# Moving the 64-row matmuls of a fused RWKV-7 and feed-forward kernel next to other 64-row work

## The chip, the cores and the metric

The kernel runs on one core of a Trainium2 chip. The metric is the device time of one execution in microseconds; for the kernel before, three runs gave 839.8, 840.27 and 841.61 us, and the median, 840.27 us, is the time before. All times of single instructions come from one profiled execution of 840.4 us.

A core has five engines with a queue each: TensorE (PE; its weight loads are listed apart as PEld), VectorE (DVE), ScalarE (ACT), GpSimd (POOL) and SyncE (SP), which here issues the DMA transfers. They meet at semaphores. Products of TensorE land in PSUM[...].

## The reference

```python
for t in range(S):                      # S = 768 steps; state is B, H, D, D = 4, 8, 40, 40
    y[:, :, t] = einsum('bhd,bhde->bhe', rt, state)
    Sa = einsum('bhde,bhe->bhd', state, at)
    state = state * wt[:, :, None, :] - einsum('bhd,bhe->bhde', Sa, bt)
    state = state + einsum('bhd,bhe->bhde', vt, kt)
x = y.transpose(0, 2, 1, 3).reshape(3072, 320)
h = x @ w_in                            # 320 x 2048
g = h * clip(h + 3, 0, 6) / 6
out = g @ w_out                         # 2048 x 320
```

The inputs r, k, v, w, a, b are fp32; the two weight matrices come in as 64-bit floats and the kernel makes fp32 of them itself.

## The kernel before, in words

**Units and groups.** The recurrence is computed in blocks of 64 steps. A *unit* is one block of one pair of batch elements, all 8 heads: 128 tokens, with the 64 steps of one batch element in partitions 0 to 63 and those of the other in 64 to 127. There are 24 units (`NK`), and four of them (`NU`: two blocks of two pairs) are a *group*. Within a block the recurrence is turned into products of small matrices: a triangular matrix of every head is inverted once per group (VectorE, lines 660 and 666, in steps that `aside` deals out), and the state of 40 x 40 per head goes from block to block. Its sums with the products of a block are the stage `sn` (matmuls in line 864, addition on VectorE in line 873).

**Stages.** `prepare` and `step` give each unit's work as stages, such as `W`, `A`, `B`, `K` (transposes), `E` and `EV` of the preparation, and `RT`, `VT`, `R`, `C`, `U`, `UT`, `rS`, `sn`, `H`, `y` of the step. A stage issues its matmuls, yields, and then issues what ScalarE, VectorE and GpSimd make of the products. From the third group on, and in the step from the second, transposes are done as *half turns*: 64 rows at a time (`turn_halves`, line 430; line 570 for the factors). Most other products of the stages use 64 rows and 64 columns of the array, or 40 rows of one such part; those of the inversion use 32 x 32 (lines 696 and 719).

**The feed-forward.** The outputs of a unit are moved by DMA into a tile `xt` of 320 features by 128 tokens, cut as 128 + 128 + 64 features. The generator `feed_forward` runs through 48 *jobs*, two for each unit, with 1024 hidden features each. A job has two parts. `expand` fills two PSUM banks `h` (c = 0 and 1, four chunks of 128 hidden features each) with 16 matmuls of 128 rows (line 968) in four pieces, and then with 8 *short* matmuls of 64 rows for the last 64 features (line 973, alternately in the upper and the lower half of the array); then ScalarE makes relu(h + 3) of each bank (line 978), and VectorE makes min of it and 6 times h (line 979, tile `gt`), which frees the bank. `contract` multiplies the result by the second weight matrix: 8 matmuls with 320 columns of output (line 992), in four pieces of two. The order is expand of one job, contract of the job before, expand of the next. There are two banks `h`, both held by one job, one bank `o` for the output and five banks `any` for the stages.

**Who sets the order.** The kernel writes its order out by hand; each engine's queue runs in it. The last loop (from the fourth unit on) goes through four rounds of stages per unit. In each, `a_block` collects the stages that are due, in two parts, and `together` issues all their matmuls in the order of the list `PRODUCTS`, then all their results in the order of `RESULTS`. The first three entries of `PRODUCTS`, `W`, `S` and `K` (the list `TURNS`), are transposes with all 128 rows; the fourth, `RT`, is a half turn. Between the parts `feed` calls `pieces(n)`, which adds up fractions and takes a whole piece from `feed_forward` whenever one is owed; a job is nine pieces, five of `expand` and four of `contract`. What is left after the last stage is taken piece by piece.

**The first group** is done differently, by `by_twos` and then by a plan written out line by line. At the same time the weights are converted in 20 pieces on VectorE and ScalarE (lines 299 to 328), and the state of the four units is summed there for the first time.

Of the kernel before, what the change touches and what calls it, by code (L numbers as in the profile page):

```python
# [16 lines left out]
P = 128  # L17
# [3 lines left out]
SLOT = 64  # L21
# [8 lines left out]
def kernel(  # L30
# [42 lines left out]
    nc = tc.nc  # L73
    B, H, T, D = r.shape
# [3 lines left out]
    NU = 2 * NP  # L78
# [12 lines left out]
    ffn = ctx.enter_context(tc.tile_pool(name="ffn", bufs=1))  # L91
# [3 lines left out]
    def bank(tag, shape, bufs):  # L95
        return ps.tile(shape, F32, name=tag, tag=tag, bufs=bufs)
# [11 lines left out]
    def ps_pair(*dims):  # L108

        n = 1  # L110
        for d in dims:
            n *= d
        if shared[0] is None or shared[1] + n > 512:
            shared[:] = [ps_any([P, 512]) for _ in range(2)], 0
        at = shared[1]
        shared[1] += n
        views, step = [], n
        for d in dims:
            step //= d
            views.append([step, d])  # L120
        return [_ap(t[:], at, views) for t in shared[0]]
# [6 lines left out]
        out=ident[:], in_=ones, pattern=[[1, P]],  # L128
# [4 lines left out]
        out=ones[:, 0:BL], in_=ones[:, 0:BL], pattern=[[1, BL]],  # L133
# [314 lines left out]
    def half(i, n=SLOT):  # L448
        return slice(SLOT * i, SLOT * i + n)
# [285 lines left out]
    def step(i):  # L735
# [117 lines left out]
                nc.scalar.activation(out=ys[:, rs::2], in_=ysp[rs], func=AF.Copy)  # L853

        def s_sn():
            sn = ps_pair(NPR, D)
            for name in "KB":
                for pr in range(NPR):
                    for s in range(2):
                        for q in range(2):  # L860
                            h = 2 * pr + s
                            by = VN[half(q), 4 * s + pr, 0:D] if name == "K" else \
                                m["U"][half(q), 4 * (s ^ q) + pr, 0:D]
                            nc.tensor.matmul(  # L864
                                out=sn[q][half(s, D), pr, :],
                                lhsT=o[name][half(q), h * D:(h + 1) * D], rhs=by,
                                start=(name == "K" and pr == 0), stop=(name == "B" and pr == NPR - 1),
                            )
            yield PE
            for q in range(2):  # L870
                for s in range(2):
                    x = st[half(s, D), q, :, 0:D]
                    nc.vector.tensor_tensor(out=x, in0=sn[q][half(s, D)], in1=x, op=ALU.add)  # L873

        def s_H():
            x = scores(m["UT"], m["RT"], swap=True)
# [58 lines left out]
    jobs = deque([(i, r) for r in range(2) for i in range(SPLIT)])  # L935
    jobs.extend((i, r) for i in range(SPLIT, NK) for r in range(2))
    sums = {}

    def available():
        if not jobs:  # L940
# [4 lines left out]
    def feed_forward():  # L945

        last = None
        while True:
            while not available():
                if last:  # L950
                    yield from contract(*last)
                    last = None
                yield None
            i, r = jobs.popleft()
            gts = []
            yield from expand(ready[i], r * NQ, gts)
            if last:
                yield from contract(*last)
            last = (i, r, gts)

    def expand(xt, j0, gts):

        hp = [bank("h", [P, NQ, P], 2) for _ in range(2)]
        for c in range(2):
            for t in range(2):
                for i in range(NQ):
                    j = c * HJ + j0 + i
                    nc.tensor.matmul(out=hp[c][:, i, :], lhsT=win[:, t, j * P:(j + 1) * P],  # L968
                                     rhs=xt[:, t, :], start=(t == 0 and i == 0), stop=False)
                yield True  # L970
        for i in range(NQ):
            for c in range(2):
                nc.tensor.matmul(out=hp[c][:, i, :],  # L973
                                 lhsT=win2[half(c), (j0 + i) * P:(j0 + i + 1) * P],
                                 rhs=xt[half(c), 2, :], start=False, stop=(i == NQ - 1))
        for c in range(2):
            gt = ffn.tile([P, NQ, P], F32, name="gt", bufs=5)
            nc.scalar.activation(out=gt[:], in_=hp[c][:], func=AF.Relu, bias=three[:], scale=1.0)  # L978
            nc.vector.scalar_tensor_tensor(out=gt[:], in0=gt[:], scalar=6.0, in1=hp[c][:],  # L979
                                           op0=ALU.min, op1=ALU.mult)  # L980
            gts.append(gt)
        yield True

    def contract(i, r, gts):
        split = i < SPLIT
        if r == 0 or split:
            op = bank("o", [P, DM], 1)
        else:
            op = sums.pop(i)
        for c in range(2):  # L990
            for n in range(NQ):
                nc.tensor.matmul(out=op[:], lhsT=gts[c][:, n, :],  # L992
                                 rhs=wout[:, c * HJ + r * NQ + n, :],
                                 start=((split or r == 0) and c == 0 and n == 0),
                                 stop=((split or r == 1) and c == 1 and n == NQ - 1))
                if n % 2 and (c == 0 or n < NQ - 1):
                    yield True
        if r == 0:
            sums[i] = op
            if split:  # L1000
                part = ffn.tile([P, 3 * P], F32, name="part", tag="xt", bufs=6)[:, 0:DM]
                nc.scalar.activation(out=part, in_=op[:], func=AF.Copy, scale=1.0 / 6.0)
                sums[i] = part
        else:
            ob = ffn.tile([P, DM], F32, name="ob", bufs=OB)
            if split:
                nc.vector.scalar_tensor_tensor(out=ob[:], in0=op[:], scalar=1.0 / 6.0,
                                               in1=sums.pop(i), op0=ALU.mult, op1=ALU.add)
# [15 lines left out]

    def pieces(n):

        owed[0] += n
        while owed[0] >= 1:
            owed[0] -= 1
            if not next(stream):  # L1030
                owed[0] = 0.0
# [180 lines left out]
    TURNS = PRODUCTS[:3]  # L1212
    WIDTH = {"R": NPR * D, "U": NPR * D, "sn": NPR * D, "EV": NPR * D}
    BLOCKS = 4

    def together(stages):

        begun, banks = [], 0

        def finish():  # L1220
            begun.sort(key=lambda x: RESULTS.index(x[0]))
            for _, rest in begun:
                for _ in rest:
                    pass
            begun.clear()
            shared[0] = None

        for name in PRODUCTS:
            for stage in stages.get(name, []):
                if name in TURNS:  # L1230
                    need = 1
                else:
                    width = WIDTH.get(name, NPR * BL)
                    need = 2 * (shared[0] is None or shared[1] + width > 512)
                if banks + need > 5:
# [42 lines left out]

    m = 0
    for i in range(NU, NK):  # L1280
        for j in range(BLOCKS):
            rate, inversion = 3.5, 0
            if i + AHEAD >= NK + NU - 1:
                rate = 4.5
            if i < 2 * NU - 1:
                rate = 2.8
            parts = a_block(m)
            next(parts)
            if side or i % NU == NU - 1 and rate < 4:
# [12 lines left out]
            m += 1  # L1302
# [36 lines left out]
```

## Time and profile before

| what | value |
|---|---|
| time, median of three runs | 840.27 us |
| TensorE busy, matmuls (both passes of each fp32 matmul) | 753.9 us, 15832 |
| VectorE / ScalarE / GpSimd busy | 549.1 / 322.6 / 158.2 us |
| line 968, the 128-row part of expand | 1536 passes, 198.1 us |
| line 973, the short part | 768 passes, 55.8 us |
| line 992, contract | 768 passes, 234.6 us |
| line 873, the state's sums | 96, 30.9 us, 321 ns each |
| TensorE busy from 0 to 160 / from 326 to 799 us | 89.9 of 160 / 472.0 of 473 us |

Busy time of TensorE is from the first start to the modelled end of matmuls that overlap each other, so a busy TensorE may still lose time between them. What a group of matmuls really costs is read from the starts: from its first start to the first start of the next group. A wait shows as idle time in front of an instruction, with the instruction on another engine that ended it.

### The profile page before, as it was taken

To read this page: it belongs to the slowest core of one execution; us is meant where nothing else is said; L and a number is where in the kernel's file an instruction comes from. 1 tells how busy PE (TensorE), PEld (TensorE's weight loads), DVE (VectorE), ACT (ScalarE), POOL (GpSimd) and SP (SyncE) were. 2 spreads that over 40 slices of the span, in tenths; PEclk is the share of its full clock that TensorE was granted. 3 is DMA by queue.
4 is the path that set the end of the run, shared out by engine and by line. 5 is a ranking of instruction groups with operands and counts; after the bars stand their busy time and mean duration, and the time that the engine had idled before them with its cause. 6 is when DMAs were issued, how large, how long until landed. Compare 5 with 4: busy or idle time off the path is not lost.

```text
span 840.4 us, 35835 instructions
## 1 busy us (share of the span) xinstructions
PE 753.9 (90%) x15832; PEld 635.5 (76%) x15832; DVE 549.1 (65%) x1112; ACT 322.6 (38%) x868; POOL 158.2 (19%) x307
## 2 busy tenths in 40 slices
PE   4722866898999998999999999999999999999998
PEld 3622766686877877888888888888888888888886
DVE  6989597887865769855589744699556675232211
ACT  1322654232265533454433545334553324322111
POOL 3231310222112230312230322022122102000000
PEclk9755576999999998999999999999999999999999
DMA  7573343331033331232321332231232101110000
GB/s 140 83 176 92 90 105 91 69 68 34 9 59 59 63 61 28 43 55 46 61 44 33 59 59 44 44 57 29 47 64 43 24 22 28 25 23 15 16 19 16
DMA packets 174218, 45.05 MB, mean 54 GB/s; under 512 B 157424, under 2 KB 172784, under 8 KB 174064
## 3 DMA queue, kind: packets, MB, share of 16 engines
q1 hardware_dynamic: 171920, 42.44, 25.7%
q8 instruction: 125, 2.05, 1.0%
q10 hardware_dynamic: 2144, 0.33, 0.2%
q14 instruction: 29, 0.24, 0.1%
HBM read 34.08 MB, written 3.93 MB: 45 GB/s over the span
## 4 chain that ended last, share of the span: by engine, by line
PE 73%; DVE 12%; issue 6%; ACT 2%; POOL 2%; DMA 2%; SPq 0%; POOLq 0%; DVEq 0%; ACTq 0%
PE o L992 23%; PE h L968 20%; PE h L973 5%; PE any L458 4%; PE any L888 3%; PE any L420 2%; PE any L430 2%; PE any L864 2%; PE any L770 1%; DVE prod L660 1%; PE any L809 1%; DVE parts L320 1%; DVE x L666 1%; PE any L830 1%; DVE score L467 1%
## 5 line engine op out<-in xcount | busy, mean ns | idle before, releaser
L992 PE MATMUL o<-wout,gt 128*128 128x320 f32 x768 | 234.6, 449 | 0.0
L968 PE MATMUL h<-xt,win 128*128 128x128 f32 x1536 | 198.1, 283 | 5.0 <-DVE gt L979 5.0
L968 PEld LDWEIGHTS h<-xt,win 128*128 128x128 f32 x1536 | 186.7, 196 | 13.9 <-DVE gt L979 5.7
L992 PEld LDWEIGHTS o<-wout,gt 128*128 128x128 f32 x768 | 139.3, 191 | 54.4 <-issue 1.4
L979 DVE SCALAR_TENSOR_TENSOR gt<-gt,h 128x512 f32<-128x512 f32 x96 | 61.3, 681 | 87.1 <-ACT gt L978 87.0
L978 ACT ACTIVATE gt<-h,three 128x512 f32<-128x512 f32 x96 | 60.8, 684 | 108.3 <-PE h L973 108.2
L903 POOL TENSOR_TENSOR yg<-ys,gam 128x512 f32<-128x512 f32 x24 | 41.4, 1726 | 182.9 <-DVE ys L900 125.5
L660 DVE TENSOR_TENSOR prod<-x 128x30 f32<-128x30 f32 (+9 forms) x180 | 61.9, 344 | 13.5 <-POOL x L651 8.1
L590 POOL TENSOR_TENSOR KBt<-K,rgt 128x320 f32<-128x320 f32 x24 | 21.2, 882 | 248.2 <-ACT rgt L580 213.2
L666 DVE TENSOR_TENSOR x<-x,prod 128x30 f32<-128x30 f32 (+9 forms) x180 | 63.3, 352 | 5.2
L873 DVE TENSOR_TENSOR state<-any,state 40x160 f32<-40x160 f32 x96 | 30.9, 321 | 47.5 <-PE any L458 26.0
L973 PE MATMUL h<-xt,win 64*128 64x128 f32 x768 | 55.8, 285 | 0.0
L467 DVE COPY_PREDICATED score<-mask,any 128x256 f32<-128x256 int32 x143 | 53.4, 437 | 1.7 <-PE any L458 1.1
L973 PEld LDWEIGHTS h<-xt,win 64*128 64x128 f32 x768 | 46.6, 187 | 5.2 <-issue 0.3
L495 DVE RECIPROCAL gam<-prods 128x256 f32<-128x256 f32 x24 | 41.5, 1741 | 13.4 <-POOL yg L903 12.1
L510 DVE RECIPROCAL rgam<-prods 128x256 f32<-128x256 f32 x24 | 41.8, 1741 | 0.0
L484 DVE TENSOR_TENSOR_SCAN prods<-wm,start 128x528 f32<-128x528 f32 x24 | 30.1, 1254 | 17.5 <-ACT wm L481 15.8
L623 ACT ACTIVATE EV<-any 64x160 f32<-64x160 f32 x92 | 24.9, 297 | 43.0 <-PE any L617 34.7
L888 PE MATMUL any<-score,KBt 64*64 64x64 f32 x1536 | 31.8, 233 | 3.5 <-DVE score L467 2.1
L888 PEld LDWEIGHTS any<-score,KBt 64*64 64x64 f32 x1536 | 27.9, 145 | 6.4 <-issue 2.4
L900 DVE TENSOR_TENSOR ys<-any,ys 128x256 f32<-128x256 f32 x44 | 16.6, 419 | 24.4 <-PE any L617 12.6
L749 ACT ACTIVATE RT<-any 128x256 f32<-128x256 f32 (+1 forms) x44 | 15.5, 401 | 42.4 <-PE any L430 42.4
(195 smaller groups left out, 1107.2 us busy)
## 6 DMA issues: line engine op xcount, KB each, us to landing
B<-in_b_dram SPq DMA_DIRECT2D x48, 80.0 KB
K<-in_k_dram SPq DMA_DIRECT2D x48, 80.0 KB
V<-in_v_dram SPq DMA_DIRECT2D x96, 40.0 KB
out_dram<-ob SPq DMA_DIRECT2D x48, 80.0 KB
R<-in_r_dram SPq DMA_DIRECT2D x92, 40.0 KB
W<-in_w_dram SPq DMA_DIRECT2D x40, 80.0 KB
A<-in_a_dram SPq DMA_DIRECT2D x40, 80.0 KB
xt<-yg SPq DMA_DIRECT2D x72, 40.0 KB
```

The source lines that it names most:

```text
L467: nc.vector.copy_predicated(out=x[:, 4 * i:4 * i + 4, :], mask=mask4, data=o[i])
L495: nc.vector.reciprocal(gv[:, :, 0:HB], o["prods"][:, :, 0, 1:HB + 1][:, :, ::-1])
L510: nc.vector.reciprocal(rv[:, :, HB:BL], o["prods"][:, :, 1, 1:HB + 1])
L660: nc.vector.tensor_tensor(out=pv, in0=_ap(x[:], (i + 1) * L + i, [[L, n], [0, i]]), in1=_ap(x[:], i * L, [[0, n], [1, i]]), op=ALU.mult,)
L666: nc.vector.tensor_tensor(out=rest, in0=rest, in1=pv, op=ALU.add)
L888: nc.tensor.matmul(out=y[q][half(s), pr, :], lhsT=o[name][half(q), h * D:h * D + SLOT], rhs=m[name][half(q), 4 * rs + 2 * s + j, :], start ...
L903: nc.gpsimd.tensor_tensor(out=yg[:], in0=m["ys"][:].rearrange("p r q t -> p r (q t)"), in1=o["G"][:], op=ALU.mult)
L968: nc.tensor.matmul(out=hp[c][:, i, :], lhsT=win[:, t, j * P:(j + 1) * P], rhs=xt[:, t, :], start=(t == 0 and i == 0), stop=False)
L973: nc.tensor.matmul(out=hp[c][:, i, :], lhsT=win2[half(c), (j0 + i) * P:(j0 + i + 1) * P], rhs=xt[half(c), 2, :], start=False, stop=(i == N ...
L978: nc.scalar.activation(out=gt[:], in_=hp[c][:], func=AF.Relu, bias=three[:], scale=1.0)
L979: nc.vector.scalar_tensor_tensor(out=gt[:], in0=gt[:], scalar=6.0, in1=hp[c][:], op0=ALU.min, op1=ALU.mult)
L992: nc.tensor.matmul(out=op[:], lhsT=gts[c][:, n, :], rhs=wout[:, c * HJ + r * NQ + n, :], start=((split or r == 0) and c == 0 and n == 0), ...
```

## The change

The 8 short matmuls of a job become a piece that can be issued at any time after `expand` has begun. `expand` counts the matmuls of each bank to know which is first and which is last, and the two results (`gt`) are issued as soon as all 24 are out. A flag `spread` is set from the eighth unit on; there the short piece has no step of its own in the stream. It is issued at the first of these: in `together`, just before `RT`, the first half turn of a round, if the round has stages; before the last piece of the contraction of the job before (`LATEST`); or after that contraction. The pacing counts 8 pieces a job in place of 9. Its purpose is that 64-row matmuls follow each other, so that TensorE changes less often between the whole array and its halves.

The second part concerns the first group only. The matmuls of `sn` use 64 columns of weights instead of 40, so that all 128 partitions of the PSUM tiles are written (rows 40 to 63 of each half hold sums that nobody reads), and VectorE adds all 128 rows with one instruction per batch element instead of two of 40 rows each.

```diff
         def s_sn():
+            wide = SLOT if i < NU else D
...
-                                out=sn[q][half(s, D), pr, :],
-                                lhsT=o[name][half(q), h * D:(h + 1) * D], rhs=by,
+                                out=sn[q][half(s, wide), pr, :],
+                                lhsT=o[name][half(q), h * D:h * D + wide], rhs=by,
...
-                for s in range(2):
-                    x = st[half(s, D), q, :, 0:D]
-                    nc.vector.tensor_tensor(out=x, in0=sn[q][half(s, D)], in1=x, op=ALU.add)
+                for rows in [slice(0, P)] if i < NU else [half(s, D) for s in range(2)]:
+                    x = st[rows, q, :, 0:D]
+                    nc.vector.tensor_tensor(out=x, in0=sn[q][rows], in1=x, op=ALU.add)
...
+    narrow, spread, LATEST = [], [False], 2
...
             if last:
-                yield from contract(*last)
+                for n, x in enumerate(contract(*last)):
+                    if n == LATEST and narrow:
+                        narrow[0]()
+                    yield x
+            if narrow:
+                narrow[0]()
             last = (i, r, gts)
...
+        def short():
+            narrow.clear()
+            for i in range(NQ):
+                for c in range(2):
+                    add(c, i, win2[half(c), (j0 + i) * P:(j0 + i + 1) * P], xt[half(c), 2, :])
+            if begun[0] + begun[1] == 6 * NQ:
+                results()
...
+        narrow.append(short)
         for c in range(2):
             for t in range(2):
                 for i in range(NQ):
                     j = c * HJ + j0 + i
-                    nc.tensor.matmul(out=hp[c][:, i, :], lhsT=win[:, t, j * P:(j + 1) * P],
-                                     rhs=xt[:, t, :], start=(t == 0 and i == 0), stop=False)
+                    add(c, i, win[:, t, j * P:(j + 1) * P], xt[:, t, :])
+                if c == 1 and t == 1 and not narrow:
+                    results()
                 yield True
...
+        if not spread[0] and narrow:
+            short()
+            yield True
...
-        owed[0] += n
+        owed[0] += n * (8 / 9 if spread[0] else 1)
...
+    FIRST_NARROW = PRODUCTS[len(TURNS)]
...
         for name in PRODUCTS:
+            if name == FIRST_NARROW and narrow and spread[0] and stages:
+                narrow[0]()
...
     for i in range(NU, NK):
+        spread[0] = i >= 2 * NU - 1
```

More of the change, by code (lines that the diff above doesn't have):

```diff
@@ L963, in expand, with add, results @@
         hp = [bank("h", [P, NQ, P], 2) for _ in range(2)]
+        begun = [0, 0]
+        def add(c, i, lhsT, rhs):
+            nc.tensor.matmul(out=hp[c][:, i, :], lhsT=lhsT, rhs=rhs, start=(begun[c] == 0),
+                             stop=(begun[c] == 3 * NQ - 1))
+            begun[c] += 1
+        def short():
[5 more added lines that the diff above has]
+                results()
+        def results():
+            for c in range(2):
+                gt = ffn.tile([P, NQ, P], F32, name="gt", bufs=5)
+                nc.scalar.activation(out=gt[:], in_=hp[c][:], func=AF.Relu, bias=three[:], scale=1.0)
+                nc.vector.scalar_tensor_tensor(out=gt[:], in0=gt[:], scalar=6.0, in1=hp[c][:],
+                                               op0=ALU.min, op1=ALU.mult)
+                gts.append(gt)
+        narrow.append(short)
         for c in range(2):
@@ L967, in expand @@
                     j = c * HJ + j0 + i
-                    nc.tensor.matmul(out=hp[c][:, i, :], lhsT=win[:, t, j * P:(j + 1) * P],
-                                     rhs=xt[:, t, :], start=(t == 0 and i == 0), stop=False)
+                    add(c, i, win[:, t, j * P:(j + 1) * P], xt[:, t, :])
+                if c == 1 and t == 1 and not narrow:
+                    results()
                 yield True
[L971 to L982, printed above, removed]
+        if not spread[0] and narrow:
+            short()
+            yield True
     def contract(i, r, gts):
```

## The prediction

> **What bounds the kernel now.** I read the page first: busy shares, then the forty slices with the granted clock.
>
> ```profile
> PE 753.9 (90%) x15832; PEld 635.5 (76%) x15832; DVE 549.1 (65%) x1112; ACT 322.6 (38%) x868; POOL 158.2 (19%) x307
> ...
> PE   4722866898999998999999999999999999999998
> ...
> PEclk9755576999999998999999999999999999999999
> ```
>
> A slice is 21 us. TensorE is less than 90% busy only in the first eight, where the weights are converted and the first group's chain runs; from about 205 us it is full, at full clock but for one dip near 320 us. A full TensorE with few waits means that from there on the time is a sum of matmul times. So I asked who TensorE waits for after 240 us:
>
> ```profile
> PE any L770 <- DVE score L467: 3.7, 1, 3.7
> PE h L968 <- DVE gt L979: 1.0, 1, 1.0
> ```
>
> Four more waits there are 0.9 us or less. In 600 us that is some 7 us of waiting; the rest must come out of the matmul stream itself. The timeline of TensorE shows where that stream loses time (columns: start, duration to the last one's end, line, tiles, rows*columns used, shape, count; the trace counts two passes for each fp32 matmul):
>
> ```profile
> 513.10 0.46 PE L570 MATMUL any<-ident,rgam 64*128 64x64 f32 x8
> 513.50 0.51 PE L864 MATMUL any<-V,KBt 64*40 64x40 f32 x32
> ...
> 515.33 1.34 PE L992 MATMUL o<-wout,gt 128*128 128x320 f32 x4
> 516.51 1.95 PE L968 MATMUL h<-xt,win 128*128 128x128 f32 x16
> 518.30 0.60 PE L420 MATMUL any<-ident,W 128*128 128x128 f32 x4
> 518.83 0.47 PE L430 MATMUL any<-ident,R 64*128 64x64 f32 x8
> 519.13 0.42 PE L430 MATMUL any<-ident,V 64*128 64x64 f32 x8
> 519.48 0.74 PE L888 MATMUL any<-score,KBt 64*64 64x64 f32 x34
> ```
>
> ```profile
> 796.74 2.05 PE L968 MATMUL h<-xt,win 128*128 128x128 f32 x16
> 798.72 1.16 PE L973 MATMUL h<-xt,win 64*128 64x128 f32 x16
> 799.81 4.57 PE L992 MATMUL o<-wout,gt 128*128 128x320 f32 x16
> 804.22 3.73 PE L968 MATMUL h<-xt,win 128*128 128x128 f32 x32
> 807.89 1.16 PE L973 MATMUL h<-xt,win 64*128 64x128 f32 x16
> 808.98 4.57 PE L992 MATMUL o<-wout,gt 128*128 128x320 f32 x16
> ```
>
> I take start-to-start times. Sixteen passes of L968 between two other 128-row groups take 518.30-516.51 = 1.79 us, 0.112 each. The same sixteen between a 64x64 group and a 64x128 group (796.74 to 798.72) take 1.98: 0.19 more. Thirty-two entered from a 128-row group and left to the 64-row L973 take 3.67 against 32 x 0.112 = 3.58: leaving costs 0.09, so entering costs 0.10. For L992: sixteen entered from L973 take 4.41, four entered from 64x64 take 1.18; twelve passes are 3.23, so 0.269 each, 4 x 0.269 = 1.08, and entering costs 0.10. L973 takes 1.09 where eight concurrent pairs at 0.112 would take 0.90: about 0.10 in, 0.09 to 0.10 out. Half turns: 8 passes 0.40, 16 passes 0.65, so 0.25 per 8, 0.14 over: 0.09 out, 0.05 in. The 128-row turns lose about 0.06 on entering. **So each change of rows or columns of the array costs 0.15 to 0.20 us**, half on the way out and half on the way in. Between L992, L968 and L420, which use the whole array, nothing is lost, though one of them is a transpose.
>
> [...] the one wait of 3.7 us is followed by a halved clock, waits up to 1.0 us after 240 us by none. [...] 32 passes of L864 with 40 columns take 0.33 us, L809 with 64 columns 0.49.
>
> **The change part by part.**
>
> (1) *The 64-row pieces.* From the eighth unit on, a job's eight short matmuls (16 passes, mode 64x128) need no longer follow its sixteen full ones. They go out just before the first half turn of a round of stages, also 64x128, or at the latest two contraction pieces before the end. I counted array modes along TensorE's instruction order of both kernels: 397 changes before, 345 after, 52 fewer; 27 of the short pieces now end directly in a half turn, and L973 is followed by L992 7 times instead of 38. By kind: 28 fewer departures from L968 x 0.094 = 2.6; 27 fewer from the short pieces x 0.097 = 2.6; 27 fewer entries to half turns x 0.05 = 1.4; 24 fewer to L992 x 0.104 = 2.5; 4 fewer to the 128-row turns x 0.056 = 0.2; 3 more departures from L992 and 3 more entries to L968 cost 0.6. Sum 8.7, take **-8.8 us** with the roundings. All of it is on the path, since TensorE is the bound there. Nowhere before does a short piece meet a half turn. Lower bound of the loss at that joint: 0, as between L968 and L420; upper bound: 0.097 + 0.05, as between modes, 27 x 0.15 = 4.0 us. I take 0, since rows and columns are equal (64*128 in both rows above).
>
> (2) *The wait near 319 us.*
>
> ```profile
> 315.27 0.41 PE L430 MATMUL any<-ident,B 64*128 64x64 f32 x8
> 319.37 1.31 PE L770 MATMUL any<-state,at 40*64 40x40 f32 x29 [3.69 <-DVE score L467]
> ```
>
> ```profile
> 315.00:326.00 11.00, 7.31 (x105) 7.01 (x104) 10.49 (x28) 0.67 (x2) 0.00 (x0) 0.69 0.25 53
> ```
>
> The second row is a stretch of 11 us with each engine's busy time. VectorE (third pair, 10.49 us) sets the wait: its queue of inversion steps delays the score that frees L770's bank. That end stays. But the new order puts four L968 matmuls and a whole short piece (0.9 + 1.1 us) ahead of L770 that came later before: **-2.0 us** of waiting. What is left, about 1.7 us, falls apart, since those four need a hidden-layer bank that VectorE frees (gt) about 1.1 us after TensorE gets there. Neither part is near 3.7 us, so the clock should not fall: from 319.4 to 325.2 it ran at half, 5.8 us for 2.9 us of work: **-2.9 us** (ends 0 and 2.9). VectorE stays full until about 350 us, so some returns: the job after next wants its hidden bank about 1.1 us before VectorE's gt frees it: **+1.1 us**. The later 1.0 us wait (L968 for gt, 558 us) has 8 us of other work between, instead of eight contraction matmuls: **-1.0 us**.
>
> (3) *The tail.* With no stages left, the last jobs send the short piece late, and only two contraction matmuls (1.1 us) stand before the next job's L968, which needs the bank that ScalarE and VectorE read. In the tail before, ScalarE's gt starts 0.1 us after the last short matmul gives way to L992 (809.08 against 808.98), and VectorE is through with the first bank 1.46 us after it (starts at 809.80, 0.64 us for one). 1.46 - 1.1 = 0.4 us, for two jobs and for the last contraction: **+1.2 us**. Everywhere else at least 5 us of TensorE work lies between, by the order of instructions; VectorE needs 2.1. The 8/9 in the pacing only replaces the ninth step; it costs nothing. Where gt now stands ahead of a stage's results in ScalarE's and VectorE's queues (four jobs), they come 1.1 us later, with 4 us and more of feed-forward before the next products.
>
> (4) *State's sums in the first group.*
>
> ```profile
> 126.50 1.32 DVE L873 TENSOR_TENSOR state<-any,state 40x160 f32<-40x160 f32 x4
> 108.64 0.55 DVE L775 TENSOR_TENSOR RR<-any,EV 128x160 f32<-128x160 f32 x2
> ```
>
> Four sums of 40 rows become two of 128 rows with the same 160 columns, and L775 shows that 128 rows take no longer. Each unit saves 1.32 - 0.6 = 0.7 us on VectorE, 4 x 0.65 = 2.6. All four sums are in the chain that ended last, between weight conversions, so most counts. Against it, weights of 64 columns: 0.16 us for 32 passes, two such per unit, 1.3 us in all, beside VectorE's queue except in the first unit, where the sum waits for them at half clock (0.6). **-1.8 us** (ends 0 and -2.6).
>
> Sum: -8.8 -2.0 -2.9 +1.1 -1.0 +1.2 -1.8 = -14.2 us. I allow 0.9 us for new waits of the size of the four small ones: 840.3 - 13.3 = **827.0 us**.
>
> **The rivals.** *A part only.* [...] the wait and the halved clock come back elsewhere in the stretch that VectorE fills (+2.0 +2.9): 831 to 832, both 836; middle 833. For it: no such joint is in the profile, and VectorE has no idle time from 315 to 350 us. Against: equal shape. *No change*: [...]: 840. For it: two banks are held longer, and TensorE has no other place to put work. Against: 5 us between in all but the last jobs. *Slower*: gt in front of stage results delays scores, and each of some 30 jobs waits 0.4 us for it as in the tail, with two falls of the clock: 30 x 0.4 + 2 x 3 - 13 = 5 above, 845. Against: VectorE is 61% and ScalarE 41% busy from 326 to 799 us (288.9 and 192.6 of 473), and TensorE waited for neither over 1.2 us there.
>
> **How the numbers follow.** Full gain 0.60, part 0.27, no change 0.05, slower 0.08. The range: below, 823.5, if the first group gives 2.6 and no new waits come; above, 835, nearly the worst of the part case. Faster 0.88, same 0.04, slower 0.08.
>
> **What would show it.** Short pieces next to L430 with 0.9 to 1.0 us per sixteen passes instead of 1.09, and L430 right behind without a loss; L968 followed by L992 at its usual pace. Near 315 us two short waits in place of one of 3.7, and no halved clock there. In the tail, waits of 0.4 us for gt before L968 and the last contraction. Two sums of 128x160 per unit in the first group, and the stretch up to 160 us shorter by 2 us. It would be wrong if short piece and half turn start with a loss of 0.15 us, or if TensorE's waits for VectorE after 326 us grow to several us.

## The result, and the profile after

The changed kernel takes 834.77 us (median of four runs, 832.4 to 836.79) against 840.15 us for the kernel before on the same chip (four runs): a ratio of 0.9932, 95% interval 0.9903 to 0.996. The gain is 5.4 us; the forecast was 13.3 us. From here on "the changed kernel" is this one, "before" the one before it. In the changed kernel the line numbers have moved: L974 is every matmul of `expand`, full or short (`128*128` or `64*128` tells them apart), L1015 is `contract`, L989 and L990 make `gt` on ScalarE and VectorE, L874 is the state's sum.

From the page of the changed kernel, the busy time of the engines and the granted clock in forty slices:

```profile
PE 746.1 (90%) x15832; PEld 631.2 (76%) x15832; DVE 546.5 (66%) x1104; ACT 322.6 (39%) x868; POOL 158.5 (19%) x307
...
PEclk8755588999999999999999999999999999999999
```

TensorE does the same 15832 passes in 7.8 us less, and the dip of the clock near 320 us is gone (granted 0.50 from 319.4 to 325.2 us before, 1.00 from 319 to 326 us now). Its waits after 240 us (us in total, times, longest):

```profile
PE h L974 <- DVE gt L990: 4.0, 5, 1.3
PE any L458 <- issue: 1.6, 3, 1.2
PE any L696 <- ACT wm L481: 1.3, 1, 1.3
PE any L617 <- issue: 1.3, 2, 1.1
PE any L770 <- DVE score L467: 0.7, 1, 0.7
```

The 3.7 us wait for the score has shrunk to 0.7, but waits for `gt`, 1.0 us before, now come to 4.0, and three other waits of over 1 us are new.

To see where the time went I cut both traces at one instruction, the first L770 of the fifth unit (235.6 us before, 228.4 after). Ahead of it the changed kernel is 7.2 us earlier in these two executions, more than the timed runs allow the first group (its part is measured below). From it to the end it takes 602.2 us against 604.8, only 2.6 less. Three more traces have one of these two orders from the cut on: 604.5 us with the old one, 603.2 and 603.4 with the new one, so the gain there is between 1 and 3 us. All short pieces that were moved lie in this second part. I then gave each group of matmuls there its shortest time for its kind and number, plus the prices of mode changes from the prediction, and summed what the starts show beyond that, waits and slow clock:

| stretch, us after the cut | before | after |
|---|---|---|
| 0 to 70 | 4.5 | 4.9 |
| 70 to 122 (the wait near 319 us and what follows) | 6.8 | 7.5 |
| 122 to 330 | 2.8 | 4.9 |
| 330 to 570 | 1.3 | 2.7 |
| 570 to the end | 0.0 | 1.0 |
| sum | 15.3 | 21.0 |

Counted in the two traces there are 52 mode changes fewer, at the prediction's prices 8.7 us (an experiment below tests the price). Waits and slow clock took 5.7 us of it back (8.7 - 5.7 = 3.0 against 2.6 measured). In the timeline of TensorE in the changed kernel (start, duration, line, tiles, size, passes, idle time before) one short piece and one of the new waits stand close together:

```profile
422.64 1.16 PE L974 MATMUL h<-xt,win 64*128 64x128 f32 x16
423.64 0.41 PE L430 MATMUL any<-ident,R 64*128 64x64 f32 x8
423.88 0.41 PE L430 MATMUL any<-ident,V 64*128 64x64 f32 x8
...
426.76 4.47 PE L1015 MATMUL o<-wout,gt 128*128 128x320 f32 x16
432.39 1.13 PE L974 MATMUL h<-xt,win 128*128 128x128 f32 x8 [1.16 <-DVE gt L990]
433.35 0.60 PE L793 MATMUL any<-ident,state 128*128 128x128 f32 x4
```

The short piece takes 423.64 - 422.64 = 1.00 us, against 1.09 before, and the half turns behind it 0.24 and 0.34 for eight passes, against 0.30 and 0.35 in the prediction's lines: the joint is free. Then 432.39 - 426.76 = 5.63 us pass from the start of sixteen passes of L1015 to the next group, in place of 16 x 0.269 = 4.30. What VectorE did in that time:

```profile
427.60 1.25 DVE L484 TENSOR_TENSOR_SCAN prods<-wm,start 128x528 f32<-128x528 f32 x1
429.94 1.75 DVE L495 RECIPROCAL gam<-prods 128x256 f32<-128x256 f32 x1 [1.10 <-POOL yg L904]
431.61 1.22 DVE L990 SCALAR_TENSOR_TENSOR gt<-gt,h 128x512 f32<-128x512 f32 x2
```

`gt`, which frees the banks, stands behind the scan (a result of the stage `W`) and the reciprocal (stage `gam`), and the reciprocal waits 1.1 us for a GpSimd instruction that reads the `gam` of an earlier unit. ScalarE had made its part by 429.6 us, so the inputs of `gt` were ready 2 us before it began, at 431.61, as the reciprocal ended (429.94 + 1.75 = 431.69). The same picture is at 309 and at 550 us: in jobs whose last four full matmuls (eight passes) are issued after a round of stages, `gt` is issued behind the round's results.

**The kernel before already had this wait, once.** Its TensorE near 558 us, the 1.0 us wait of the prediction:

```profile
552.69 4.57 PE L992 MATMUL o<-wout,gt 128*128 128x320 f32 x16
558.25 1.16 PE L968 MATMUL h<-xt,win 128*128 128x128 f32 x8 [0.98 <-DVE gt L979]
```

and its VectorE there:

```profile
555.17 1.75 DVE L495 RECIPROCAL gam<-prods 128x256 f32<-128x256 f32 x1 [1.10 <-POOL yg L903]
...
557.51 1.28 DVE L979 SCALAR_TENSOR_TENSOR gt<-gt,h 128x512 f32<-128x512 f32 x2
```

The same scan, the same reciprocal, the same wait for GpSimd ahead of `gt`. The change did not remove this wait; it made three of one.

Why were 309 and 432 us free of it before? VectorE had the same scan, wait and reciprocal there. The kernel before at the place that is 432 us in the changed one:

```profile
434.72 4.57 PE L992 MATMUL o<-wout,gt 128*128 128x320 f32 x16
439.13 0.60 PE L793 MATMUL any<-ident,state 128*128 128x128 f32 x4
...
441.39 3.84 PE L968 MATMUL h<-xt,win 128*128 128x128 f32 x32
```

```profile
437.20 1.75 DVE L495 RECIPROCAL gam<-prods 128x256 f32<-128x256 f32 x1 [1.10 <-POOL yg L903]
...
439.54 1.28 DVE L979 SCALAR_TENSOR_TENSOR gt<-gt,h 128x512 f32<-128x512 f32 x2
```

Here 2.3 us of the next round's matmuls stand between the contraction and the next job's first L968, and `gt` is done with the first bank (half of 1.28 us after 439.54) before 441.39. In the changed kernel the short piece no longer stands ahead of the contraction, and the next job's first matmuls come ahead of that round (L793 follows them, at 433.35), so TensorE wants the bank earlier by both. It is the same at the place of 309 us: in the kernel before, L793 follows the contraction at 314.44 and the next L968 comes at 321.61.

### The profile page after: what moved, and what is told of

Its sections match the earlier page's. It is cut to its first block, busy times and chain, and to the rows that moved or that the text cites. A ratio compares the mean times of both kernels' runs of the same rounds, so it can differ in the third digit from the quotient of the medians.

```text
span 830.6 us, 35844 instructions
## 1 busy us (share of the span) xinstructions
PE 746.1 (90%) x15832; PEld 631.2 (76%) x15832; DVE 546.5 (66%) x1104; ACT 322.6 (39%) x868; POOL 158.5 (19%) x307
## 4 chain that ended last, share of the span: by engine, by line
PE 64%; DVE 15%; issue 10%; ACT 4%; POOL 3%; DMA 1%; SPq 0%; POOLq 0%; DVEq 0%; ACTq 0%
PE h L974 22%; PE o L1015 20%; PE any L458 3%; PE any L889 3%; DVE prod L660 2%; DVE x L666 2%; PE any L420 2%; PE any L430 2%; PE any L865 2%; PE any L770 1%; PE any L809 1%; DVE parts L320 1%; DVE score L467 1%; PE any L830 1%; PE any L846 1%
## 5 line engine op out<-in xcount | busy, mean ns | idle before, releaser
L974 PE MATMUL h<-xt,win 128*128 128x128 f32 (+1 forms) x2304 | 253.2, 284 | 5.5 <-DVE gt L990 5.5
L974 PEld LDWEIGHTS h<-xt,win 128*128 128x128 f32 (+1 forms) x2304 | 232.8, 193 | 24.4 <-issue 9.0
L1015 PE MATMUL o<-wout,gt 128*128 128x320 f32 x768 | 232.5, 445 | 0.2 <-DVE gt L990 0.2
L1015 PEld LDWEIGHTS o<-wout,gt 128*128 128x128 f32 x768 | 138.7, 191 | 51.1 <-issue 1.0
L989 ACT ACTIVATE gt<-h,three 128x512 f32<-128x512 f32 x96 | 62.0, 686 | 104.6 <-PE h L974 104.3
L990 DVE SCALAR_TENSOR_TENSOR gt<-gt,h 128x512 f32<-128x512 f32 x96 | 61.5, 677 | 61.3 <-ACT gt L989 61.3
L660 DVE TENSOR_TENSOR prod<-x 128x30 f32<-128x30 f32 (+9 forms) x180 | 62.8, 349 | 13.5 <-POOL x L651 8.1
L874 DVE TENSOR_TENSOR state<-any,state 40x160 f32<-40x160 f32 (+1 forms) x88 | 27.9, 321 | 62.7 <-PE any L865 36.5
L666 DVE TENSOR_TENSOR x<-x,prod 128x30 f32<-128x30 f32 (+9 forms) x180 | 65.0, 361 | 5.6 <-DVE prod L660 0.3
L729 ACT ACTIVATE tinv<-any 32x256 f32<-32x256 f32 (+1 forms) x56 | 19.3, 344 | 30.6 <-PE any L719 29.8
L775 DVE TENSOR_TENSOR RR<-any,EV 128x160 f32<-128x160 f32 x44 | 12.2, 318 | 27.2 <-PE any L458 26.3
```

Of the source, the lines that this page charges most:

```text
L660: nc.vector.tensor_tensor(out=pv, in0=_ap(x[:], (i + 1) * L + i, [[L, n], [0, i]]), in1=_ap(x[:], i * L, [[0, n], [1, i]]), op=ALU.mult,)
L666: nc.vector.tensor_tensor(out=rest, in0=rest, in1=pv, op=ALU.add)
L974: nc.tensor.matmul(out=hp[c][:, i, :], lhsT=lhsT, rhs=rhs, start=(begun[c] == 0), stop=(begun[c] == 3 * NQ - 1))
L1015: nc.tensor.matmul(out=op[:], lhsT=gts[c][:, n, :], rhs=wout[:, c * HJ + r * NQ + n, :], start=((split or r == 0) and c == 0 and n == 0), ...
```

## Experiments

Each kernel ran on one chip beside the kernel before, and each ratio is to that.

| kernel | median us | before, same chip | ratio, 95% interval |
|---|---|---|---|
| sums only | 836.76 | 840.58 | 0.9961, 0.9949 to 0.9973 |
| pieces only | 839.0 | 840.58 | 0.9982, 0.9974 to 0.999 |
| pieces only, none moved during the inversion | 839.75 | 840.58 | 0.9994, 0.9984 to 1.0004 |
| before, 96 mode changes more | 857.47 | 840.58 | 1.0201, 1.0188 to 1.0215 |
| changed, gam's results later | 827.88 | 840.29 | 0.9854, 0.9837 to 0.9872 |
| the same, and the old order in the tail | 829.11 | 840.29 | 0.9849, 0.9828 to 0.9869 |
| changed, nine pieces a job | 907.74 | 840.29 | 1.0799, 1.0783 to 1.0815 |
| changed, old order in the tail | 834.15 | 840.29 | 0.9915, 0.99 to 0.993 |
| before, gam's results later | 839.23 | 840.68 | 0.9982, 0.9976 to 0.9989 |
| changed, whole sums in two units of four | 838.23 | 840.68 | 0.9966, 0.9951 to 0.9982 |
| as "and the old order in the tail", inversion dealt out slower | 859.08 | 840.68 | 1.0228, 1.0205 to 1.0251 |

**The two parts apart.** First the kernel before with the new `s_sn` alone, everything of the feed-forward as it was:

```diff
+            wide = SLOT if i < NU else D
...
-                for s in range(2):
+                for rows in [slice(0, P)] if i < NU else [half(s, D) for s in range(2)]:
```

> The kernel before with the wide sums of the state in the first group alone; the short pieces stay where they were. Theory A (the 52 saved mode changes are worth 8.7 us, as read from the rows, and about 6 us of them come back as waits of TensorE for VectorE in the stretches where an inversion runs): the sums give what their lines show, four times 0.65 us less on VectorE, so 837 to 838.5. Theory B (most of the measured gain comes from the first group[...]): 833 to 835.5.

Measured 3.8 us faster (interval 2.3 to 4.3), more than the 1.8 forecast for it; 836.76 lies between the two theories, 0.2 us from A. Then the changed kernel with the old `s_sn`:

```diff
-            wide = SLOT if i < NU else D
...
-                for rows in [slice(0, P)] if i < NU else [half(s, D) for s in range(2)]:
+                for s in range(2):
```

> The changed kernel with the sums of the first group as before; only the short pieces move. Theory A: 8.7 us less for mode changes, some 6 us more of waits: 836.5 to 838. Theory B: within 1 us of the kernel before, 839 to 840.5, or more.

Measured 1.6 us faster, at the edge of theory B and 1.0 us outside theory A. The two gains add up to the whole, 3.8 + 1.6 = 5.4. So most of the gain does come from the first group, as theory B had it; why so much of it comes from there isn't shown by this. The part that was to bring 11.5 us brings 1.6, and the failure lies there. In its trace the stretch after the cut takes 603.2 us against 604.8, with 22.0 us of waits and slow clock.

**The price of a mode change.** In the kernel before, the last matmul of each bank's second half goes between the fourth and the fifth short matmul, so that every short piece is cut in two:

```diff
-                for i in range(NQ):
+                for i in range(NQ - t):
...
         for i in range(NQ):
+            if i == NQ // 2:
+                for c in range(2):
+                    j = c * HJ + j0 + NQ - 1
+                    nc.tensor.matmul(out=hp[c][:, NQ - 1, :], lhsT=win[:, 1, j * P:(j + 1) * P],
+                                     rhs=xt[:, 1, :], start=False, stop=False)
```

> The kernel before with two of the sixteen full matmuls of each job put between the fourth and the fifth short one: the same matmuls, 96 mode changes more (493 instead of 397), no other edit. If a change costs what the rows show, 0.094 + 0.100 us, 96 x 0.195 = 18.7 us more, 857 to 860. If a change costs less in the whole than in the rows, because waits absorb it, under 850.

Same matmuls, 96 changes more (two for each of 48 jobs): 16.9 us slower, 16.9 / 96 = 0.176 us each, within the 0.15 to 0.20 read from the profile. Its TensorE timeline shows the price in place:

```profile
651.70 0.72 PE L978 MATMUL h<-xt,win 64*128 64x128 f32 x8
652.35 0.71 PE L975 MATMUL h<-xt,win 128*128 128x128 f32 x4
```

Eight short passes take 0.65 us from start to start, where half of an uncut piece of sixteen takes 0.55. So 8.7 us for 52 changes is a sound price (52 x 0.176 = 9.2, though some of the 52 are of kinds that this kernel doesn't add); the gain was lost elsewhere.

**Is the region near 319 us the loser?** The changed kernel with the old `s_sn`, and without moved pieces while an inversion is dealt out:

```diff
-            if name == FIRST_NARROW and narrow and spread[0] and stages:
+            if name == FIRST_NARROW and narrow and spread[0] and stages and not side:
...
-        if not spread[0] and narrow:
+        if (not spread[0] or side) and narrow:
...
-        owed[0] += n * (8 / 9 if spread[0] else 1)
+        owed[0] += n * (8 / 9 if spread[0] and not side else 1)
```

> As the pieces alone, but while an inversion is under way the short piece stays at the end of expand, as before. 372 mode changes instead of 345 (before: 397), 12 short pieces beside a half turn instead of 27. Theory A: 25 x 0.17 = 4.2 us less for mode changes, the waits for the hidden bank at 308, 432 and 549 us and for the inverse at 345 us are gone, that of 3.7 us at 319 us is back with its halved clock, the tail costs 1 us: about 837, no slower than with all pieces moved. If the gain goes with the number of changes alone and waits do not matter, it is half of that of all pieces moved.

0.8 us faster than before (the interval includes none), about half of what pieces only gave, as the second expectation had it; but the two intervals overlap. (Its one profiled execution takes 606.2 us after the cut, no less than before, so only the timed runs speak for a gain.) The wait for the score was back at 3.75 us, against 3.69 in the kernel before; the `gt` waits outside the tail were gone. Other waits stood in its trace, of L458 (0.7 us at 489 and 0.9 at 608) and of L719 (0.8 at 385). So the pieces moved during the inversion do remove the wait near 319 us, and they are also what brings the `gt` waits. Leaving them out is no clear net gain: the 837 of theory A was missed.

**The order of gt and gam.** If the new waits come from `gam`'s results (the reciprocal, and three copies on GpSimd) ahead of `gt` on VectorE, issuing these results half a round later must take them away. The scan belongs to the stage `W` and stays where it was. The changed kernel with:

```diff
+    late = []
...
         for k, part in enumerate(parts):
+            for stage in late:
+                for _ in stage():
+                    pass
+            late[:] = part.pop("gam", [])
             together(part)
```

> The changed kernel, with the results of the stage gam (reciprocal of the decay, 1.75 us, and the 1.1 us that it waits for GpSimd) issued half a round later, after the feed-forward pieces of that half, so that gt no longer stands behind them in VectorE's queue. 345 mode changes as in the changed kernel. Theory A (the waits for the hidden bank come from what stands ahead of gt in VectorE's queue): the three waits of 1.3 to 1.5 us fall below 0.4 each, 3 to 4 us less: 831 to 832. Theory C (VectorE as a whole is the bound in the stretches with an inversion, so a wait removed comes back at the next product that needs VectorE): as the changed kernel within 0.8 us, 834 to 835.5.

Measured 827.88 us, below what either theory expected. TensorE and VectorE of this kernel, at the place of the wait at 432 us:

```profile
424.81 4.47 PE L1015 MATMUL o<-wout,gt 128*128 128x320 f32 x16
429.11 1.05 PE L974 MATMUL h<-xt,win 128*128 128x128 f32 x8
```

```profile
427.14 1.28 DVE L990 SCALAR_TENSOR_TENSOR gt<-gt,h 128x512 f32<-128x512 f32 x2 [0.26 <-ACT gt L989]
...
430.89 1.75 DVE L495 RECIPROCAL gam<-prods 128x256 f32<-128x256 f32 x1
```

`gt` starts 3.7 us ahead of the reciprocal, and sixteen passes of L1015 take 4.30 us: no wait. Over the run the waits for `gt` fall from 4.0 to 0.4 us. From the cut to the end the trace takes 597.4 us, 4.8 less than the changed kernel: 3.6 from `gt` and, by an estimate from the starts, 1.5 from a stretch of halved clock near 346 us that this execution didn't have (eight passes of L974 take 1.00 us there, 1.87 in the changed kernel); waits of L458 rose by 1.0 (2.6 against 1.6), and smaller ones fell.

Does the later `gam` help by itself? The same edit in the kernel before:

> The kernel before, with one change: the results of the stage gam (scan, reciprocal) are issued half a round later, after the feed-forward's pieces. Theory A (the gain of 7 us that this gave on the changed kernel is the removal of gt's waits, which the changed kernel has and the kernel before nearly lacks): here only the 1.0 us wait at 558 us and part of the 3.7 us wait at 319 us can shrink, 837 to 840. Rival theory D (issuing gam's results later is worth some 7 us by itself, and has nothing to do with the short pieces): 833 to 834.

1.45 us faster; the 0.98 us wait at 558 us is gone (its contraction takes 4.41 us, the 3.7 us wait stays). Theory D is out. What the edit is worth with the moved pieces is read from two kernels described next, which ran on one chip and differ in it alone: 829.11 against 834.15 us, 5.0 us. From the cut on their traces take 596.2 and 599.8 us; the difference is 3.6 us, which is what the `gt` waits of the slower one come to, and in both the eight passes of L974 near 346 us take the 1.0 us of full speed. The rest of the 5.0 lies ahead of the cut in these two executions and isn't explained. So the edit does most of its work where the pieces have moved.

**The tail.** The changed kernel with `spread[0] = False` ahead of the last loop, so that the last jobs have the old order:

```diff
+    spread[0] = False
     while jobs or next(stream):
```

> The changed kernel with the short piece at the end of expand for the jobs after the last stage, nothing else. Two waits of 0.38 us before L974 and one of about 0.2 us before the last contraction go: 1.0 us less than the changed kernel, 833.5 to 834. Any theory that puts the loss elsewhere expects the same here; if it is more than 2 us the tail holds more than the trace shows.

834.15 us. In the trace the tail's excess of 0.99 us falls to 0.01, as forecast; that is too small for the timing to tell (the two intervals overlap widely). Both edits together:

> As the run before, and besides the last jobs, those after the last stage, issue the short piece at the end of expand as in the kernel before. Theory A: 1.0 us less than the run before it, 830 to 831. Theory C: 833 to 834.5.

829.11 us, not to be told from 827.88; in the trace, from the cut to the end 596.2 us against 597.4. These two kernels are the fastest of the study, 1.5% under the kernel before. An estimate for the pieces follows from the medians: 11.2 us of gain in all, less 3.8 for the sums and 1.45 for `gam`'s order by itself, leaves about 6 us, against 1.6 with the old order of `gam` and the new tail. The 8.7 us of mode changes still don't come in whole.

**Is the pacing neutral?** The changed kernel without the 8/9:

```diff
-        owed[0] += n * (8 / 9 if spread[0] else 1)
+        owed[0] += n
```

> The changed kernel without the factor 8/9 in the pacing, so that each round is followed by 9/8 of the feed-forward work. 354 mode changes (17 short pieces beside a half turn instead of 27). If the waits come from TensorE reaching VectorE's results too early because less feed-forward work lies between, they shrink by more than the 9 changes cost (1.6 us), 832 to 834. If not, 1.6 us more than the changed kernel or worse, since the feed-forward runs out of units earlier: 836 to 839.

907.74 us, 73 us more than with it; no theory had that. From its waits after 240 us:

```profile
PE h L974 <- DMA xt<-yg: 40.3, 12, 6.5
```

A job now has eight pieces, so the feed-forward ran ahead at the old pace, overtook the recurrence and waited for units that weren't finished. The factor is needed. Something like it happens if the inversion's steps are dealt out two to a piece in place of three in the second group (on the kernel with both edits; the line stands at two places):

```diff
-                rate, inversion = 6.2, 2 + (i < 2 * NU)
+                rate, inversion = 6.2, 2
```

> The changed kernel with gam's results issued half a round later and the pieces at the end in the old order, and with the inversion's steps dealt out two to a piece in the second group too, where it was three. Theory A (VectorE, filled by these steps, sets the waits that are left near 312 and 317 us): these two waits of 1.2 and 1.1 us go, 826.5 to 828.5, against 829. Rival (steps dealt out later move the wait to where the inversion's end is needed, after 350 us): a wait of 1 to 4 us there, 829 to 833.

859.08 us, 30 more than without it. From its waits after 240 us:

```profile
PE h L974 <- DMA xt<-yg: 8.2, 4, 2.8
PE any L696 <- DVE tb L669: 7.3, 1, 7.3
```

The two waits near 312 and 317 us are gone, as the first theory said, but the end of the inversion comes late and TensorE waits 7.3 us for it. The rate of 6.2 pieces lasts as long as the inversion, so the feed-forward overtakes the units as well. The rival was right in kind, and its size far too small.

**Whole sums in half of the units.**

```diff
-            wide = SLOT if i < NU else D
+            wide = SLOT if i < NP else D
```

(and the same condition for the sums)

> The changed kernel, with the whole sums of state (128 rows) only in the first two of the first group's four units. Theory A (each unit's shorter sum brings its own part of the 3.8 us): half of it is lost, 836.2 to 837.2. Rival (the gain comes from one place, where a stretch of halved clock falls away, and not from each sum): the same as the changed kernel, 834.5 to 835.2, or all of it lost, 838 to 839.

838.23 us, 2.45 faster than before. That lies where the rival had "all of it lost", and outside theory A; but with an interval of 1.5 to 4.1 us for the gain, against 2.3 to 4.3 for the sums alone, the timing doesn't settle how the gain splits. The traces speak for theory A. From the first state sum near 90 us to that of the fourth unit it takes 62.0 to 63.7 us in five kernels with the old sums, 61.5 in this one, and 58.1 to 60.7 in seven with all sums whole; the means are 62.8, 61.5 and 59.5. Taken apart, the stretch from the first sum to the second is 12.2 us in this kernel (old 12.8 to 13.1, whole 11.5 to 12.1), from the second to the third 23.0 (old 23.3 to 23.4, whole 22.3 to 23.1), and from the third to the fourth, where its sums are old, 26.3 (old 25.8 to 27.3, whole 23.6 to 25.7): it is short where its own sums are whole.

## Why the prediction was right in direction and wrong in size

Two steps failed. In the sum the larger is (2): -3.8 us were forecast for the stretch near 319 us, and it lost 0.7. The other is the sentence in (3) that at least 5 us of TensorE work lie between a job's last matmul of `h` and the next job's first, against 2.1 us that VectorE needs: in the jobs of the three `gt` waits the work was 4.3 to 5.1 us and the need 5.4 to 6.5. One of the waits that it missed lies in the stretch of (2).

**(1) The 64-row pieces, -8.8: right.** 52 changes fewer were counted in the traces too, the joint of short piece and half turn is free (1.00 us for the short piece), and the price is confirmed by the kernel with 96 more (0.176 us each). (The latest place of a short piece is one contraction piece of two matmuls before the end, not two pieces as (1) says; (3) has it right. And TensorE's row of the page has an 8 in two later slices, near 200 and 325 us.)

**(2) The wait near 319 us, -2.0 -2.9 +1.1 = -3.8: wrong, +0.7.** The 3.7 us wait went, as said. The step took the 1.7 us that were left to be all, and only one hidden-bank wait of 1.1 to return. What came in the same stretch:

```profile
312.76 0.94 PE L770 MATMUL any<-state,at 40*64 40x40 f32 x29 [0.73 <-DVE score L467]
...
317.52 0.67 PE L617 MATMUL any<-V,score 64*64 64x40 f32 x30 [1.06 <-issue]
...
345.33 1.01 PE L696 MATMUL any<-tb,F 32*32 32x32 f32 x64 [1.32 <-ACT wm L481]
346.28 2.08 PE L974 MATMUL h<-xt,win 128*128 128x128 f32 x8
348.15 1.06 PE L793 MATMUL any<-ident,state 128*128 128x128 f32 x4
```

In this timeline of the changed kernel TensorE waits 0.73 us for the score, 1.06 before L617 (the profile names no releaser; VectorE masks the next score from 316.99, and the bank behind it is the likely one), and 1.32 for the inversion's products, where before there were none. The `gt` wait of 1.3 us at 309 stands ahead of them. And the clock fell here after all: eight passes of L974 from 346.28 to the next group at 348.15 take 1.87 us, against 8 x 0.112 = 0.90, at a granted clock of 0.50. Three of six traces with this wait don't have the halved clock; without it the stretch would be about 1.5 us better by an estimate from the starts, and still 3 us short of the forecast. VectorE was busy almost without a gap up to 341 us (30.2 us of the 32 from 309 on) as it was before (29.3 of the same 32): TensorE, with its work earlier, met its results at other places. Even the wait for ScalarE's `wm` leads there, since the copies in front of it had waited 3.0 us for the inversion's last step on VectorE:

```profile
341.59 2.12 ACT L681 ACTIVATE tinv<-tb 32x1024 f32<-32x1024 f32 x2 [3.04 <-DVE tb L669]
```

With the inversion dealt out more slowly the waits at 312 and 317 us went, which speaks for VectorE as their cause. The prediction said "VectorE stays full until about 350 us, so some returns", and put 1.1 on it where the whole gain returned.

**The later wait, -1.0: wrong.** "Has 8 us of other work between" was read from the short piece's place, not from where `gt` is issued. The wait is still there, 1.15 us at 550, and has company at 309 and 432.

**(3) The tail, +1.2: right,** 0.99. **"Everywhere else at least 5 us of TensorE work lies between, by the order of instructions; VectorE needs 2.1": the other step that failed.** Between the last matmul of `h` and the next job's first there are 4.3 us in the jobs of 432 and 550 us (16 x 0.269), and VectorE needs 2.1 only with an empty queue, as in the tail it was read from. With ys, scan, the wait for GpSimd and the reciprocal ahead it needs 432.2 - 426.8 = 5.4 (to the end of `gt` for the first bank, half of 1.22 us after 431.61). In the job of 309 us a stage stands between, so the work is 5.1 us, and the need 6.5. The step also looked at the jobs in which `gt` moves *ahead* of stage results, and not at those in which it stays behind them. The allowance of 0.9 us for new waits was for these; in the stretches from 122 to 330 and from 330 to 570 us past the cut they and others grew by 2.1 and 1.4. Of these 3.5 us the longest single wait outside `gt` is one of L458 at 600 us (1.2). The profile names no releaser for it, and the waits of L458 grew when `gt` was issued earlier; what sets them stays open. **"The 8/9 costs nothing"** held for the changed kernel, but as one that must be there.

**(4) State's sums, -1.8: right in kind, too small, -3.8.** The price per unit was read too low. VectorE in the changed kernel and in the kernel before:

```profile
124.30 0.55 DVE L874 TENSOR_TENSOR state<-any,state 128x160 f32<-128x160 f32 x2
124.76 0.68 DVE L320 SCALAR_TENSOR_TENSOR parts<-raw_tt,parts 128x512 uint32<-128x512 uint32 x1
```

```profile
109.11 1.46 DVE L325 TENSOR_SCALAR raw<-raw 128x512 uint32<-128x512 uint32 x1
...
127.85 0.69 DVE L320 SCALAR_TENSOR_TENSOR parts<-raw_tt,parts 128x512 uint32<-128x512 uint32 x1
```

The next instruction starts 0.46 us after the first sum, where before (126.50 in the prediction's line) it started 1.35 after it. That is 0.9 us a unit, where the prediction took 0.65 from the durations: the records of the 128-row sums overlap each other and the next instruction by 0.08 us, those of the 40-row sums don't. L775, two instructions of the same size, showed it in the kernel before: it starts at 108.64, and the next instruction at 109.11, 0.47 us later. Four units give 3.6 us, close to the 3.8 measured. I also took off 0.6 for wider weights and called most, not all, of the saving on the path. The stretch between the sums of units one and four holds three of them, 2.7 us; it became 3.3 shorter on average, with a spread of 2 us between executions. The granted clock differs there too (from 126.5 to 137 us it averaged 0.70 before and 0.94 after, but 0.67 in the kernel with sums only), so it isn't what all these kernels have in common.

**The rivals.** "A part only", 833, came nearest, and for one of its reasons: waits and a halved clock came back in the stretch that VectorE fills. The other loss in its sum, 4.0 us at the joint of short piece and half turn, is refuted: the short piece takes 1.00 us there, against 1.09 before. "No change", with two banks held longer, came nearest to what took most: waits for hidden banks, 4.0 us against 1.0 before. What I held against it, "5 us between", was the unsound number. The queue that the slower rival spoke of, VectorE's, was the right one, but three jobs of some thirty met it.

The measured 834.8 lies inside the range, whose upper end, 835, was "nearly the worst of the part case"; that is no merit of the sum, whose terms for the waits failed. With `gt` ahead of the reciprocal the kernel takes 827.9 us. That this is close to the forecast of 827.0 is partly chance, since the sums gave 2 us more and the stretch near 319 us less than was forecast.

## What to carry to other kernels

Work taken out of a full engine was gained here only as far as the buffers that feed it came free earlier too. For every instruction that frees a bank, read the queue in front of it at that place, with what its neighbours wait for; its duration in an idle stretch is not the time it needs (2.1 us in the tail, 5.4 to 6.5 in the jobs that waited). Read too which matmul wants the bank next in the new order: a piece that moves away pulls the next one forward. A small wait in the profile before, here 1.0 us, is worth following to its cause before an edit is priced: it shows a slack that is already gone, and a tighter order may repeat it. And price an instruction by the time to the start of the next one, not by its duration: two sums of 128 rows saved 0.9 us a unit where the durations gave 0.65.

## What the runs showed of the hardware

The halved clock near 346 us followed a wait of only 1.32 us, with 32-row matmuls behind it. Six of the traces have this wait, of 1.27 to 1.32 us. In three of them the eight passes of L974 behind it take 1.5 to 1.9 us (1.87 in the changed kernel, at a granted clock of 0.50), and in three 1.0 us, full speed; in the kernel with `gam`'s results later, for example, 345.13 - 344.13 = 1.00. What decides between the two isn't shown here; a wait near 3.7 us was not needed. I had taken "not near 3.7 us" for safe.

Two sums of 128 rows free VectorE for the next instruction after 0.46 us, four of 40 rows with the same columns after 1.35. What makes the 40-row sums follow each other without overlap isn't shown here.

Executions of the same first group differ by 2 us or more (58.1 to 60.7 above), which is as large as the effects sought there: one profiled execution doesn't measure them, the timed runs do.
